# The last stretch of a fused attention and soft-MoE kernel, with its value products, transposes and one polynomial chain in another order

## The chip, the core and the metric

The kernel runs on one core of one Trainium2 chip. A core has five engines that work side by side, each through its own queue in program order: TensorE (PE in the profile; its weight loads, PEld, overlap its products), VectorE (DVE), ScalarE (ACT), GpSimd (POOL) and SyncE (SP), which only issues transfers. They wait for each other by semaphores. Data lies in SBUF (128 partitions) and matrix products land in PSUM, 8 banks of 2 KB a partition. The metric is the device time of one execution in microseconds (us); the kernel before takes 281.48, the median of 3 runs (281.21 to 282.12).

## What is computed

```
scores = q @ k.T / sqrt(64)                 # 8 batches x 12 heads, 448 x 448
scores = cap * tanh(scores / cap)           # cap = 30
attn   = softmax(scores) @ v
x      = attn, heads side by side           # 3584 rows x 768
logits = x @ phi                            # 3584 x 32 slots (8 experts x 4)
slot_input = softmax(logits, over rows).T @ x
slot_out   = relu(slot_input @ w1[e]) @ w2[e]     # per expert, 768 -> 1024 -> 768
out    = softmax(logits, over slots) @ slot_out
```

The slot sums go over all rows, so no expert product can start before the last head's attention is done; and all 11 MB of the output follow the experts.

## The kernel before, in words

**Attention.** Heads go in pairs, 0 to 47, and two pairs make a quad. Scores are kept transposed: a tile is 64 keys of both heads of a pair (128 partitions) by 448 queries, and a pair has 7 tiles. All 336 tiles stand in one list and are worked off in 56 chunks of 6. For a chunk j the PE makes scores (`qk_chunk`, in two halves of 3 tiles), ScalarE makes tanh of each half (`tanh_chunk`) and one exp over the chunk (`exp_chunk`). For many chunks the first tiles' exp is done on VectorE instead, by a polynomial of seven steps (`poly_exp`, L602 to L609); the table `SHARED` says how many tiles (one for chunk 54), the table `POLY` at which slot each step is issued. The steps of a chunk depend on each other in order.

Value products (`pv_mms`, L613 to L629) take exp tiles as stationary operand and the values, with a column of ones, as moving one. The 448 queries are 3 groups of 128 and a rest of 64. The groups are products of form 128\*128; the rest goes as two products of form 64\*64, one per head ("tail products"). `norm` (L631) divides by the sums (a reciprocal, then a multiply, both VectorE) into `xq`. `x_transp` (L682) transposes a pair's `xq` on PE into a PSUM tile `xps` (3 transposes of form 128\*128, 2 of form 64\*64; there is one buffer for all users of `psT`) and copies it to `xT`. `phi_last` (L960) multiplies `xT` with phi into the logits `lpl` (again 3 of full form, and for the rest two of form 128\*64).

**Order.** The order on every engine is written out by hand. Each chunk j of the main loop (L893 on) has named slots ("0", "m", "e", "a", "b", "r", "c", "d"), each with a "<" part before and a ">" part after; `at(j, slot, f, ...)` puts a piece of work in one. `spare` and `busy` are PE products of ones without use for the result. The last chunk, 55, takes exp in three pieces, of 3, 2 and 1 tiles (L930 to L932).

**The end.** `TAILSEQ` (L991) is the order of what follows the main loop: "m" and "mt" are pair 46's group and tail products (into `pvm`), "nm" its normalization, "l" and "lt" pair 47's group and tail products (into `pvl`, two halves: groups 0 and 1, and group 2 with the rest), "n" the normalization of such a half, "x45" and "x46" those pairs' transposes (x46 with its copy on ScalarE), "p" phi products of a range of pairs. With CM = 2, tile CM of pair 46 is the one whose exp is the polynomial of chunk 54. C1, C2, C3 = 1, 4, 6: pair 47's tile 0 is in chunk 54, tiles 1 to 3, 4 to 5 and 6 belong to the three exp pieces. `turns` (L941) gives the PSUM banks in order of use. Then `x_last` transposes pair 47's two halves into `xpl`, `phi_last` adds the last phi products, `e_last` takes exp of the logits in two halves, `slot_mms` makes the slot sums, and `layer1` (L1064) begins the experts.

**Transfers.** SyncE's queue first loads values, then 21 parts of w2 (`w2t`, L1049) into memory that attention has given up, then stores the output (L1126).

Of the kernel before, what the change touches and what calls it, by code (L numbers as in the profile page):

```python
# [10 lines left out]
BF16 = mybir.dt.bfloat16  # L11
# [7 lines left out]
P = 128  # L19
HP = 64  # L20
NT = 7
# [16 lines left out]
def kernel(  # L38
# [12 lines left out]
    B, H, _, _ = q.shape  # L51
# [11 lines left out]
    NQ = B * NQB  # L63
# [6 lines left out]
    pe, dve, act, pool, sp = nc.tensor, nc.vector, nc.scalar, nc.gpsimd, nc.sync  # L70
# [3 lines left out]
    psT = ctx.enter_context(tc.tile_pool(name="psT", bufs=1, space=PSUM))  # L74
# [301 lines left out]
    def exp_chunk(j):  # L376
# [199 lines left out]
            (54, '<a'): ((53, 4),),  # L576
            (54, '<b'): ((54, 0), (53, 5)),
            (54, '>b'): ((54, 1),),
            (54, '>c'): ((53, 6),),
            (55, '0'): ((54, 2),),  # L580
            (55, 'e'): ((54, 3),),
            (55, '<a'): ((54, 4),),
            (55, '>a'): ((54, 5), (54, 6))}
    shared = dict(SHARED)

    octaves = cap * math.log2(math.e)
# [73 lines left out]
    def pv_tail(pr, c0, c1):  # L660

        pv_mms(pr, c0, c1, (NF,), pvs[pr][:, 2 * NF:NT, :])
# [125 lines left out]
    def at(j, slot, f, *a):  # L788
        if j < 0:
            j, slot = 0, "b"  # L790
        aux.setdefault((j, slot), []).append((f, a))
# [9 lines left out]
    def quad_in(Q, cast_k, cast_q, k_in, q_in, v_in):  # L801
        if 0 < Q < NQ:
            for nm, when in (("k", cast_k), ("q", cast_q)):
                at(*when, *((cast, nm) if Q == 1 else (load, nm, Q + 1)))
            at(*k_in, transp, "k", Q)
            at(*q_in, transp, "q", Q)
            if Q == 1:
                for n in range(2):
                    at(*v_in, vcast, Q, n)
# [6 lines left out]
    for b in range(B):  # L816
        j, p = b * PER, 6 * b

        def when(nm):
            return j + WHEN[nm][0], WHEN[nm][1]  # L820

        if b == 0:
            quad_in(1, (0, "c"), (0, "c"), (0, "d"), (0, "d"), (2, "d"))
        else:
            quad_in(3 * b + 1, *(when(x + "1") for x in ("lk", "lq", "k", "q", "v")))
        for n in (2, 3):
            quad_in(3 * b + n, *(when(f"{x}{n}") for x in ("lk", "lq", "k", "q", "v")))
        if b == 0:
            at(j + 1, "d", spare, 14)
            at(j + 2, "d", spare, 5)  # L830
        for k, slot, f, n in FILL:
            if (b or k > 2) and j + k < NCH - 1:
                at(j + k, slot, f, n)
        for hq in range(NQB if b < B - 1 else 1):
            at(*when(f"x{hq}"), x_transp, NQB * b + hq)
        if b == B - 1:
            at(j + 6, "a", x_transp, NQ - 2, (0,))
        if b < B - 1:
            at(*when("lg"), logits, b)
            at(*when("ee"), e_exp, b)  # L840
            at(*when("ss"), slot_sums, b)
            if b < B - 2:
                at(*when("et"), e_transp, b)
            if b % 2:
                at(*when("es"), e_sums, b // 2)
# [4 lines left out]
        at(1 + n * (NCH - 5) // len(wjobs), "b", *job)  # L850
    for j, slot, n, parts in ((0, "a", 5, 1), (0, "c", 16, 3), (1, "b", 12, 3), (1, "c", 3, 1)):
        at(j, slot, spare, n, parts)
    LATE = ((52, 'd', 3, 1), (54, 'd', 3, 3),)
    for j, slot, n, parts in LATE:
        at(j, slot, spare, n, parts)
    at(34, "<b", fill, 7)
# [15 lines left out]
    def busy(n, home=None, by=None):  # L872
        home, by = junk if home is None else home, ones if by is None else by
        if home.shape[-1] > P:
            for _ in range(n // 3):
                pe.matmul(home, ones, wide, start=True, stop=True)
            n, home = n % 3, home[:, 0:P]
        for _ in range(n):
            pe.matmul(home, by, by, start=True, stop=True)
# [47 lines left out]
    last = NPAIR - 1  # L927
# [10 lines left out]
    attp.close()  # L938
    mid = ExitStack()
    big = mid.enter_context(tc.tile_pool(name="big", bufs=1, space=PSUM, reuse_waits="tile"))  # L940
    turns = [0, 1, 2, 6, 3, 4, 5, 0, 6, 0, 1, 2, 3, 6, 5, 4, 0, 1, 2, 6, 3, 0, 1, 2, 6, 5]  # L941

    def bank(shape, dt=F32, name="bank"):
        n = turns.pop(0)
        return big.tile(shape, dt, name=name, tag=f"b{n}")
# [9 lines left out]
    CM = sum(place[last - 1, c] < NTILE - 2 * CH for c in range(NT))  # L955

    def pv_last(c0, c1, half, tails=(False, True)):
        pv_mms(last, c0, c1, halves[half], pv2[half], tails)

    def phi_last(pr, gs, done=False):  # L960
        Q, h = divmod(pr, 2)
        for g in gs:
            phi_mms(lps[g // 2][:, g % 2, :], xTs[Q][:, h, :], g, pr % NJ,
                    pr == last - 5 and g % 2 == 0, done)

    def tail_step(what, *a):
        if what == "m":
            pv_mms(last - 1, *a, (0, 1, 2), pvs[last - 1])
        elif what == "mt":
            pv_tail(last - 1, *a)  # L970
        elif what == "nm":
            norm(last - 1, 0, NT, pvs.pop(last - 1))
        elif what == "x45":
            x_transp(NQ - 2, (1,))
        elif what == "x46":
            x_transp(NQ - 1, (0,), act.copy)
        elif what == "l":
            pv_last(*a, (False,))
        elif what == "lt":
            pv_last(*a, 1, (True,))  # L980
        elif what == "p":
            for gs in ((0, 1, 2), (NF,)):
                for pr in range(*a):
                    phi_last(pr, gs)
        elif what == "n":
            norm(last, cuts[a[0]], cuts[a[0] + 1], pv2[a[0]])
        else:
            run(NCH - 1, what)

    C1, C2, C3 = NT - CH, NT - CH + CL, NT - 1  # L990
    TAILSEQ = (("m", 0, CM), ("m", CM, NT), ("l", 0, C1, 0), ("x45",), ("mt", CM, NT),  # L991
               ("mt", 0, CM), ("l", 0, C1, 1), ("l", C1, C2, 0), ("p", last - 5, last - 1), ("l", C2, C3, 0),
               ("nm",), ("l", C3, NT, 0), ("l", C2, C3, 1), ("l", C3, NT, 1), ("l", C1, C2, 1),
               ("x46",), ("lt", C3, NT), ("n", 0), ("lt", C2, C3), ("lt", C1, C2),
               ("lt", 0, C1), ("n", 1))
    for step in TAILSEQ:
        tail_step(*step)
    assert not aux, aux.keys()

    el = consts.tile([P, NG, NS], BF16, name="E", tag="E", bufs=2)  # L1000
    es[bl] = el
    xpl = [bank([P, 2 * P], BF16, name="xpl"),
           psT.tile([P, 2 * P], BF16, name="xpl", tag="T")]
    zl = bank([P, NS], name="zps")

    def x_last(s, copy):
        q0, q1 = 2 * s * P, min(2 * s * P + 2 * P, S)
        turn_x(xpl[s], q0, last, halves[s])
        copy(xTs[NQ - 1][:, 1, q0:q1], xpl[s][:, 0:q1 - q0])

    def e_last(s):
        act.activation(el[:, 2 * s:2 * s + 2, :], lps[s], ACT.Exp)

    busy(1)
    x_last(0, act.copy)
    busy(3)
    phi_last(last - 1, (0, 1, 2))
    x_last(1, dve.tensor_copy)
    phi_last(last, (0, 1), True)
    busy(6)  # L1020
    e_last(0)
    phi_last(last, (2,))
    phi_last(last - 1, (NF,))
# [150 lines left out]
    for n in range(B // 2 * NT):  # L1174
        bb, c = divmod(n, NT)
# [59 lines left out]
```

## Time and profile before

| | |
|---|---|
| median of 3 runs | 281.48 us (281.21 to 282.12) |
| span of the profiled execution | 279.2 us (the page does not give its whole time) |
| busy: PE, DVE, ACT, POOL | 247.0, 239.1, 248.6, 142.0 us |
| last exp piece of attention ends | 235.40 us |
| first expert product | 239.63 us |
| first store issued | 249.98 us |
| granted clock, 228 to 270 us | 1.00 |

One execution is profiled; times are counted from its first instruction. In rows in order of time the columns are start, time from the first start to the last end, engine, line, operation, tiles written and read, form and shape, count, and in brackets the idle time before it and what ended it. Rows of the same kind that follow each other are merged. A matmul's row ends when its result is there; the next one may issue long before.

### The profile page before, as it was taken

The page shows a single profiled execution, that of the slowest core. Times are in us where ns is not written, and L with a number is a line of the kernel's source. Part 1 is how long each engine was busy: PE and PEld are TensorE (multiplying, and loading weights), DVE is VectorE, ACT ScalarE, POOL GpSimd, SP SyncE. Part 2 cuts the span into 40 slices and gives each one's busy share as a digit, 9 for nine tenths or more (in the row PEclk, how much of TensorE's full clock was granted, in tenths as well). Part 3 has the DMA queues.
Part 4 walks back from the last instruction along what each step waited for, and adds up shares of the span by engine and source line. Part 5 has one row for each costly group of instructions (what it writes and reads, how often), then busy time and mean ns, then how long its engine had stood idle before and what let it go on. Part 6 is the DMA issues. An engine that isn't in the chain of part 4 may idle for free.

```text
span 279.2 us, 10421 instructions
## 1 busy us (share of the span) xinstructions
PE 247.0 (88%) x4560; PEld 166.6 (60%) x4560; DVE 239.1 (86%) x473; ACT 248.6 (89%) x195; POOL 142.0 (51%) x198
## 2 busy tenths in 40 slices
PE   8898989998999999989999999899999999998720
PEld 7555556756675766566756675657566678553300
DVE  3479999999999999999999999999999997347940
ACT  4999999999999999999999999999999998237720
POOL 8796548662957296728673758375743230200000
PEclk9999999999999999999999999999999999999995
DMA  6999999999999999999999999999999588979997
GB/s 197 277 193 202 219 219 234 229 221 219 224 225 220 219 229 226 225 217 229 223 226 212 213 219 231 218 210 215 231 217 215 117 279 293 367 290 383 434 424 312
DMA packets 57340, 68.08 MB, mean 244 GB/s; under 512 B 4048, under 2 KB 53840, under 8 KB 56784
## 3 DMA queue, kind: packets, MB, share of 16 engines
q0 software_dynamic: 42448, 35.31, 80.0%
q1 hardware_dynamic: 14704, 32.02, 32.6%
q8 instruction: 35, 0.57, 0.7%
q10 hardware_dynamic: 144, 0.10, 0.1%
q14 instruction: 9, 0.07, 0.1%
HBM read 91.72 MB, written 19.27 MB: 398 GB/s over the span
## 4 chain that ended last, share of the span: by engine, by line
ACT 38%; DVE 27%; PE 27%; issue 3%; POOL 1%; ACTq 0%; DVEq 0%
ACT ex L366 15%; ACT ex L374 15%; PE pv L627 8%; ACT ex L362 6%; DVE xq L637 4%; PE sc L349 3%; DVE xp L605 3%; DVE xp L607 3%; DVE ex L608 2%; DVE ex L602 2%; PE so_ps L1098 2%; PE hp L1070 2%; DVE xf L604 2%; DVE ex L609 2%; DVE xp L606 2%
## 5 line engine op out<-in xcount | busy, mean ns | idle before, releaser
L366 ACT ACTIVATE ex<-sc 128x1344 f16<-128x1344 f32 (+1 forms) x87 | 112.9, 1402 | 0.9 <-PE sc L349 0.9
L374 ACT ACTIVATE ex<-ex 128x1344 bf16<-128x1344 f16 (+5 forms) x58 | 110.7, 1916 | 0.1
L627 PE MATMUL pv<-vbd,ex 128*128 128x130 bf16 (+1 forms) x1610 | 94.0, 212 | 7.6 <-POOL vbd L289 3.4
L627 PEld LDWEIGHTS <-ex 128*128 128x128 bf16 (+1 forms) x1680 | 75.6, 101 | 34.9 <-issue 6.2
L289 POOL CAST vbd<-vraw 64x896 bf16<-64x896 f32 x46 | 47.3, 1028 | 57.3 <-PE pv L627 35.7
L349 PE MATMUL sc<-qT,kT 64*64 64x448 bf16 x672 | 66.0, 359 | 6.7 <-ACT ex L366 4.8
L362 ACT ACTIVATE ex<-sc 128x2688 f16<-128x2688 f32 x13 | 33.6, 2586 | 0.0
L349 PEld LDWEIGHTS <-kT 64*64 64x64 bf16 x672 | 22.1, 105 | 16.3 <-ACT ex L366 6.9
L637 DVE TENSOR_TENSOR xq<-pv,rec 128x448 bf16<-128x448 f32 x46 | 28.7, 625 | 1.6
L607 DVE TENSOR_TENSOR xp<-xp,xf 128x1344 f16<-128x1344 f16 (+2 forms) x34 | 27.1, 798 | 0.6
L608 DVE TENSOR_TENSOR ex<-ex,xp 128x1344 uint16<-128x1344 uint16 (+2 forms) x34 | 26.9, 791 | 0.2
L605 DVE TENSOR_TENSOR xp<-xf 128x1344 f16<-128x1344 uint16 (+2 forms) x34 | 26.8, 789 | 0.2
L116 POOL DMA_DIRECT2D w1b<-in_moe_w_dram x32 | 26.3, 825 | 0.0
L602 DVE TENSOR_SCALAR ex<-ex 128x1344 uint16<-128x1344 f16 (+2 forms) x34 | 17.0, 500 | 1.4 <-ACT ex L366 0.8
L606 DVE TENSOR_SCALAR xp<-xp 128x1344 f16<-128x1344 f16 (+2 forms) x34 | 17.2, 505 | 0.6
L281 DVE COPY kT<-kps 128x896 bf16<-128x896 bf16 x23 | 14.2, 617 | 4.0 <-PE kps L276 2.8
L297 POOL MEMSET vbd<- 64x1 bf16 x22 | 2.8, 129 | 28.6 <-PE pv L627 28.3
L604 DVE TENSOR_SCALAR xf<-ex 128x1344 uint16<-128x1344 uint16 (+2 forms) x34 | 16.7, 491 | 0.4
L185 POOL DMA_DIRECT2D qb<-in_q_dram x22 | 16.3, 740 | 1.2 <-PE qps L279 0.5
L609 DVE TENSOR_SCALAR ex<-ex 128x1344 uint16<-128x1344 uint16 (+2 forms) x34 | 16.4, 483 | 0.4
L120 POOL DMA_DIRECT2D w2d<-in_moe_w_dram x21 | 16.4, 816 | 0.0
L185 POOL DMA_DIRECT2D kb<-in_k_dram x22 | 16.3, 739 | 0.0
(124 smaller groups left out, 320.2 us busy)
## 6 DMA issues: line engine op xcount, KB each, us to landing
w1b<-in_moe_w_dram POOLq DMA_DIRECT2D x32, 384.0 KB, 10.2
vraw<-in_v_dram SPq DMA_DIRECT2D x44, 224.0 KB, 6.2
w2d<-in_moe_w_dram POOLq DMA_DIRECT2D x21, 384.0 KB, 9.9
w2t<-w2d SPq DMA_DIRECT2D x21, 384.0 KB, 6.2
qb<-in_q_dram POOLq DMA_DIRECT2D x22, 224.0 KB, 8.2
kb<-in_k_dram POOLq DMA_DIRECT2D x22, 224.0 KB, 8.1
w2b<-in_moe_w_dram POOLq DMA_DIRECT2D x11, 384.0 KB, 9.5
out_dram<-ob SPq DMA_DIRECT2D x2, 1536.0 KB, 7.7
```

The costliest lines, as they stand in the source:

```text
L116: pool.dma_start(out=w1b[e][:, js, fs], in_=w1r[:, e, js, fs])
L185: pool.dma_start(out=t, in_=quad_ap(nm, Q))
L289: pool.tensor_copy(vbds[Q % 2][r, :, :, c0:c0 + DH], raw[r])
L349: ins = pe.matmul(sc[cs, u, 0:S], qkT["k", Q][r, c, cs], qkT["q", Q][r, :, cs], start=True, stop=True).ins
L362: apart["t", i - 1] = apart["t", i] = act.activation(exs[j].bitcast(F16), own["board"][:, :, 0:S], ACT.Tanh, scale=qk_scale / cap).ins
L366: ins = act.activation(exs[j][:, half * CS + u0:half * CS + u1, :].bitcast(F16), (own[0] if i == u0 == 0 else sc)[:, u0:u1, 0:S], ACT.Tanh ...
L374: act.activation(exs[j][:, u0:u1, :], exs[j][:, u0:u1, :].bitcast(F16), ACT.Exp, scale=cap)
L605: lambda: dve.tensor_tensor(p, s, s.bitcast(F16), op=ALU.mult),
L607: lambda: dve.tensor_tensor(p, p, s, op=ALU.mult),
L608: lambda: dve.tensor_tensor(y, y, p, op=ALU.add),
L627: pe.matmul(out_, exs[j][r, u, q0:q0 + (HP if tail else P)], v_, start=(c == 0 and g == gs[0] < NF), stop=(c == NT - 1), skip_group_check= ...
L637: dve.tensor_tensor(xq[Q][:, h, s0:s1, :], pv[:, 0:s1 - s0, 0:DH], rec.to_broadcast([P, s1 - s0, DH]), op=ALU.mult)
```

## The change

- The last polynomial step of chunk 53 and those of chunk 54 are issued one or two slots sooner; pair 44's transposes come after pair 45 instead of between its products.
- The spare product at (54, 'd') is left out, and of `busy(1)`, `busy(3)`, `busy(6)` at the end only one `busy(1)` stays, at another place.
- `TAILSEQ` is new: pair 46's polynomial tile is last of its group products; pair 46's normalization comes before pair 47's later products; pair 47's tail products go in two groups (tiles 0 to 3, then 4 to 6); x46 and the phi products come at the end. The phi products of pairs 44 and 45 are issued between the two `x_last`.
- `x_last(0)` copies on VectorE and `x_last(1)` on ScalarE instead of the reverse; the second `xpl` is in bank 3 instead of the `psT` buffer.

```
-            (54, '>c'): ((53, 6),),
-            (55, '0'): ((54, 2),),
-            (55, 'e'): ((54, 3),),
-            (55, '<a'): ((54, 4),),
-            (55, '>a'): ((54, 5), (54, 6))}
+            (54, '<c'): ((53, 6), (54, 2)),
+            (54, '>c'): ((54, 3),),
+            (55, '0'): ((54, 4),),
+            (55, 'e'): ((54, 5),),
+            (55, '<a'): ((54, 6),)}
...
-            at(j + 6, "a", x_transp, NQ - 2, (0,))
+            at(j + 6, "t0", x_transp, NQ - 2, (0,))
...
-    LATE = ((52, 'd', 3, 1), (54, 'd', 3, 3),)
+    LATE = ((52, 'd', 3, 1),)
...
-    turns = [0, 1, 2, 6, 3, 4, 5, 0, 6, 0, 1, 2, 3, 6, 5, 4, 0, 1, 2, 6, 3, 0, 1, 2, 6, 5]
+    turns = [0, 1, 2, 6, 3, 4, 5, 0, 3, 6, 0, 1, 2, 3, 6, 5, 4, 0, 1, 2, 6, 3, 0, 1, 2, 6, 5]
...
-    TAILSEQ = (("m", 0, CM), ("m", CM, NT), ("l", 0, C1, 0), ("x45",), ("mt", CM, NT),
-               ("mt", 0, CM), ("l", 0, C1, 1), ("l", C1, C2, 0), ("p", last - 5, last - 1), ("l", C2, C3, 0),
-               ("nm",), ("l", C3, NT, 0), ("l", C2, C3, 1), ("l", C3, NT, 1), ("l", C1, C2, 1),
-               ("x46",), ("lt", C3, NT), ("n", 0), ("lt", C2, C3), ("lt", C1, C2),
-               ("lt", 0, C1), ("n", 1))
+    TAILSEQ = (("m", 0, CM), ("m", CM + 1, NT), ("m", CM, CM + 1), ("l", 0, C1, 0), ("x45",),
+               ("mt", 0, NT), ("nm",), ("l", 0, C1, 1), ("l", C1, C2, 0), ("l", C1, C2, 1),
+               ("lt", 0, C2), ("l", C2, C3, 0), ("l", C2, C3, 1), ("l", C3, NT, 0), ("n", 0),
+               ("l", C3, NT, 1), ("lt", C2, NT), ("n", 1), ("x46",), ("p", last - 5, last - 3))
...
-    xpl = [bank([P, 2 * P], BF16, name="xpl"),
-           psT.tile([P, 2 * P], BF16, name="xpl", tag="T")]
+    xpl = [bank([P, 2 * P], BF16, name="xpl") for _ in range(2)]
...
+    x_last(0, dve.tensor_copy)
+    tail_step("p", last - 3, last - 1)
+    x_last(1, act.copy)
+    phi_last(last - 1, (0, 1, 2))
+    phi_last(last, (0, 1), True)
     busy(1)
-    x_last(0, act.copy)
-    busy(3)
-    phi_last(last - 1, (0, 1, 2))
-    x_last(1, dve.tensor_copy)
-    phi_last(last, (0, 1), True)
-    busy(6)
     e_last(0)
     phi_last(last, (2,))
```

## The prediction

> **What bounds the kernel now.** I read the head of the page, then the engines' busy time stage by stage, then each engine's rows in order of time from the last stretch of attention to the first expert product, and last the store queue. Times are microseconds from the span's start; the columns of the stages are the stretch, its length, busy time (instructions) of PE, weight loads, VectorE, ScalarE, GpSimd, then granted clock, DMA share, GB/s.
>
> ```profile
> span 279.2 us, 10421 instructions
> 229.70:232.25 2.55, 2.49 (x43) 1.87 (x42) 2.48 (x7) 2.55 (x3) 0.03 (x1) 1.00 0.91 309
> 232.25:235.40 3.15, 3.15 (x75) 2.89 (x72) 2.17 (x7) 3.15 (x4) 0.00 (x0) 1.00 0.85 280
> 235.40:239.63 4.23, 4.21 (x84) 3.12 (x82) 1.72 (x7) 1.32 (x5) 0.18 (x1) 1.00 0.89 309
> 239.63:250.00 10.37, 10.37 (x228) 5.95 (x228) 4.77 (x18) 2.91 (x5) 1.63 (x1) 1.00 0.91 359
> 260.00:270.00 10.00, 5.29 (x26) 2.26 (x24) 7.45 (x9) 5.84 (x7) 0.00 (x0) 1.00 1.02 426
> ```
>
> ScalarE is busy 2.55 of 2.55 and 3.15 of 3.15 until 235.40: it sets the pace of attention's last stretch. From 235.40 it is idle two thirds of the time and a chain through PE, VectorE and ScalarE sets the pace, with PE issuing nearly throughout (4.21 of 4.23). From 239.63 PE alone does (10.37 of 10.37), until stores begin; then the DMA engines are full (1.02). The pieces that the change touches lie between these rows:
>
> ```profile
> 234.72 0.68 ACT L374 ACTIVATE ex<-ex 128x448 bf16<-128x448 f16 x1
> 234.67 0.46 PE L694 MATMUL lpl<-phib,xT 128*128 128x32 bf16 x12
> 235.06 0.30 PE L698 MATMUL lpl<-phib,xT 128*64 128x32 bf16 x8
> 235.29 0.86 PE L627 MATMUL pvl<-vbd,ex 128*128 128x130 bf16 x12
> 235.99 0.33 PE L675 MATMUL xps<-ident,xq 128*128 128x128 bf16 x3
> 236.25 0.22 PE L680 MATMUL xps<-ident,xq 64*64 64x64 bf16 x2
> 236.30 0.39 PE L627 MATMUL pvl<-vbd,ex 64*64 64x65 bf16 x14
> 235.84 0.18 DVE L634 RECIPROCAL rec<-pvl 128x4 f32<-128x4 f32 x1 [0.53 <-PE pvl L627]
> 236.06 0.42 DVE L637 TENSOR_TENSOR xq<-pvl,rec 128x256 bf16<-128x256 f32 x1
> 236.73 0.18 DVE L634 RECIPROCAL rec<-pvl 128x3 f32<-128x3 f32 x1 [0.24 <-PE pvl L627]
> 236.94 0.36 DVE L637 TENSOR_TENSOR xq<-pvl,rec 128x192 bf16<-128x192 f32 x1
> 237.36 0.23 PE L675 MATMUL xpl<-ident,xq 128*128 128x128 bf16 x1
> 237.52 0.22 PE L680 MATMUL xpl<-ident,xq 64*64 64x64 bf16 x2
> 237.78 0.26 DVE L1009 COPY xT<-xpl 128x192 bf16<-128x192 bf16 x1 [0.48 <-PE xpl L680]
> 238.09 0.19 PE L694 MATMUL lpl<-phib,xT 128*128 128x32 bf16 x1
> 238.49 0.22 ACT L1012 ACTIVATE E<-lpl 128x64 bf16<-128x64 f32 x1 [0.35 <-PE lpl L698]
> 239.63 4.07 PE L1070 MATMUL hp<-w1b,slT 128*32 128x512 bf16 x72
> ```
>
> So the last exp piece ends at 234.72 + 0.68 = 235.40. The path from it: last value products, the tail products (236.30 to 236.69), normalization of the last half (236.73 to 237.30), its transposes (237.36 to 237.74), VectorE's copy (to 238.04), the last phi products (238.09), exp of the logits (to 238.71), slot sums, and the first expert product at 239.63, which is 4.23 after the exp. Everything before 235.40 counts only if it delays PE beyond that moment.
>
> ```profile
> L1098 PE MATMUL so_ps<-w2t,hpad x84: 326/326/336, 247.4 to 252.9; 128*32 128x384 bf16 x84
> L1049 SPq DMA_DIRECT2D w2t<-w2d x21: 319/371/1539, 222.2 to 242.5; - x21
> DMA to landing us min/median/max: 3.0/6.2/8.5
> 249.98 8.86 SPq L1126 DMA_DIRECT2D out_dram<-obh  x16
> ```
>
> Does a shift at 239.63 reach the end? The last w2t load is issued at 242.5 and lands by 242.5 + 8.5 = 251.0 at the latest; its products are the last of the 84, near 252.9, so PE does not wait for it. The first store, at 249.98, follows PE's work; from then on the stores run at full DMA share. A shift under about 1 us is thus passed on one for one, sooner or later.
>
> **The change part by part.** First the two prices. A 130-column value product issues every (0.86 - 0.23) / 11 = 0.058, taking one matmul's 0.23 off its row of 12; a phi product every (0.46 - 0.19) / 11 = 0.025; a pair of tail products about (0.39 - 0.22) / 6 = 0.03. A change of form (full rows to 64 rows or columns, or back): the 3 transposes at 235.99 should issue in 0.17, and the next form begins after 0.26, so 0.09; the 12 phi products 0.30, after 0.39, again 0.09; the 8 narrow ones, in pairs 0.035 apart, 0.14, after 0.23, again 0.09.
>
> The Trainium skill, "TensorEngine Tiling (Array Packing)", section "Tiling Modes", says that a change of tiling mode drains the TensorE. The rows agree that a change costs, 0.09 each; by a full drain, taken as one matmul's 0.22, it would be more than twice that, which is the second rival below.
>
> *Product left out, spare at (54, 'd').*
>
> ```profile
> 229.75 0.34 PE L876 MATMUL junk<-ones 128*128 128x384 bf16 x1
> 230.14 0.90 PE L627 MATMUL pv<-vbd,ex 128*128 128x130 bf16 x12
> 229.07 0.62 DVE L637 TENSOR_TENSOR xq<-pv,rec 128x448 bf16<-128x448 f32 x1
> ```
>
> Pair 45's products can start at 229.69 + 0.06 = 229.75 instead of 230.14: 0.39 sooner on PE. ScalarE is the bound there, so this is worth 0 by itself.
>
> *Polynomial steps one place sooner, pair 44's transposes after pair 45.*
>
> ```profile
> 231.29 0.39 DVE L607 TENSOR_TENSOR xp<-xp,xf 128x448 f16<-128x448 f16 x1
> 231.59 0.38 DVE L689 COPY xT<-xps 128x448 bf16<-128x448 bf16 x1
> 231.90 0.38 DVE L608 TENSOR_TENSOR ex<-ex,xp 128x448 uint16<-128x448 uint16 x1
> 232.50 0.20 DVE L634 RECIPROCAL rec<-pv 128x7 f32<-128x7 f32 x1
> 232.74 0.62 DVE L637 TENSOR_TENSOR xq<-pv,rec 128x448 bf16<-128x448 f32 x1
> ```
>
> VectorE runs the same operations; the copy of pair 44 (0.31 of the queue) goes behind pair 45's normalization, and L608 then follows L607 directly, which I price at +0.12 (L608 to its dependent successor L609 is 0.41 against the 0.30 from L607 to the copy). So the reciprocal is at 232.50 - 0.31 + 0.12 = 232.31, xq ends near 233.17 and the copy near 233.47. Pair 45's transposes use the same PSUM tile, so PE is held there until 233.47 + 0.06 = 233.53 (now they run near 233.6). From there to the last piece PE has: transposes 0.22, 14 tail products 0.21, 10 value products 0.58, 8 tail products 0.12, 6 value products 0.35, and 5 changes 0.45, sum 1.93, ready at 235.46. The exp piece releases PE at about 235.45. So this part costs 0, with no reserve: every 0.1 that VectorE is later there is 0.1 later at the end. I bound it by 0 and +0.2 (half of that 0.41).
>
> *Order behind the last exp.* From 235.45 on PE issues: 3 value products 0.17, 6 tail products 0.10, pair 46's transposes 0.22, phi of pairs 42 and 43 0.22, first transposes of pair 47 0.12, phi of 44 and 45 0.22, one transpose 0.06: 1.11 of work, and 9 changes of form, 0.81. The last pair of transposes then issues at 235.45 + 1.92 = 237.37 (now 237.52). VectorE is no longer what is late: the last half's tail products issue by 235.80 and end by 236.0, the first half's normalization (0.18, 0.42) occupies VectorE from 235.76 (its last product, issued at 235.51, ends by 235.73) to about 236.35, so the second ends near 236.90 instead of 237.30 and waits 0.3 for PE. The phi products, 0.44 plus four changes 0.36, were under ScalarE's exp before; now they stand on PE's path and eat most of the 0.40 won. The junk between (L876, L879) goes and had filled waits; it is worth 0.
>
> *Copies exchanged.*
>
> ```profile
> 236.51 0.53 ACT L689 COPY xT<-xps 128x448 bf16<-128x448 bf16 x1 [1.10 <-PE xps L680]
> 237.00 0.37 ACT L1009 COPY xT<-xpl 128x256 bf16<-128x256 bf16 x1
> ```
>
> The last copy, 192 columns, moves from VectorE (0.26) to ScalarE: between 0.37 at 256 columns and 0.53 at 448 the slope gives 0.32; bounds 0.26 and 0.37. So: last transposes end 237.37 + 0.22 = 237.59, copy 237.63 to 237.95, phi at 238.00 instead of 238.09. The second xpl in a bank of its own frees it from pair 46's copy; both bank owners (pvm, pvl) have been read by then, so 0. Behind 238.00 nothing changes.
>
> Sum: 0 + 0 - 0.09 = -0.09 at the first expert product, hence at the end. The profiled execution's whole time is not on the page; the median stands 281.48 - 279.2 = 2.3 above the span, which I take as what lies around it. Forecast 281.48 - 0.09 = 281.39, so 281.4.
>
> **The rivals.**
> *PE is lighter than I sum* (form changes partly hidden behind weight loads): then VectorE's result decides, the single transpose issues at 236.96 instead of 237.36, and with 0.06 given back by the slower copy the gain is 0.34: 281.1. For it: weight loads are busy only 3.12 of 4.23; against it: the three rows all showed 0.09. It also bounds the gain of this order: the rest of the path is unchanged.
>
> *PE's queue behind the last exp becomes the bound* (slower). Twelve changes of form stand from the exp to the slot sums instead of six, nine of them ahead of the last transposes. If a change where the next operand also comes fresh costs a whole result time, 0.22, then 9 x 0.13 = 1.17 is added, less 0.09: +1.08, 282.6. It decides from 0.10 a change upward, and passes +0.84 from 0.19. For it: the new changes sit between very short groups (2 to 6 products), which no row shows in such density. Against it: 0.09 thrice.
>
> *The clock falls without the junk* (slower): the 4.07 of L1070 would at worst double, 285.5. Against it: between 260 and 270 PE is busy only 5.29 of 10 and the clock is 1.00. By the Trainium skill, "TensorE: Matmul & The Clock Gate", section "Part 1: The HAM clock gate", an idle window of about 3.4 us halves the clock; no gap of that length arises here.
>
> *It doesn't reach the end.* If the w2t stream, landing up to 251.0, rather than the store at 249.98 sets the start of the stores, any gain is lost: 281.5.
>
> **How the numbers follow.** My forecast has 0.50 (its own range 281.1 to 281.7), lighter PE 0.13, lost gain 0.13, PE's queue 0.11, the clock 0.03. The other 0.10 is for a gain outside this path, which I can't name: this order yields 0.34 at most. A difference of 0.3%, 0.84, is about what a measurement of this kernel can tell from none. Same: 0.50 + 0.13 + 0.13 = 0.76; slower 0.11 + 0.03 = 0.14; faster 0.10. The range, with the runs' own 281.21 to 282.12 and half of the queue's case, is 280.8 to 282.3; it leaves out the unnamed gain, the clock and the worse half of the queue's case, some 0.19.
>
> **What would show it.** Right: L374's last piece still ends near 235.4; VectorE's last xq ends near 236.9; the last L680 pair issues near 237.4, with PE and not VectorE as what it followed; the last copy is on ScalarE with 0.32; L1070 begins near 239.5 and the first store near 249.9. Wrong: L374's last piece ends elsewhere (then something reaches ScalarE that I did not see); gaps over 0.15 at changes of form (second rival); pair 45's L675 later than 233.7 (the shared PSUM tile); a clock below 1.00 before 270; or the first store's shift not found again in the span.

## The result, and the profile after

The changed kernel takes 282.45 us, the median of 22 runs (281.87 to 285.57); the kernel before, run beside it, 281.7 (22 runs, 280.76 to 282.56). The ratio is 1.0037, 95% interval 1.0022 to 1.0052. The change makes the kernel slower by a third of a per cent, about 1 us, where 281.4 and no measurable difference had been forecast.

The rows of the changed kernel's trace that answer to those of before, each engine's in order of time (its line numbers are smaller by 3 from `layer1` on: L1067 was L1070, L1095 was L1098, L1123 was L1126):

```profile
232.93 2.73 ACT L374 ACTIVATE ex<-ex 128x1344 bf16<-128x1344 f16 x3
236.81 0.36 DVE L637 TENSOR_TENSOR xq<-pvl,rec 128x192 bf16<-128x192 f32 x1
237.73 0.22 PE L680 MATMUL xpl<-ident,xq 64*64 64x64 bf16 x2
237.99 0.32 ACT L1007 COPY xT<-xpl 128x192 bf16<-128x192 bf16 x1 [0.72 <-PE xpl L680]
239.90 5.59 PE L1067 MATMUL hp<-w1b,slT 128*32 128x512 bf16 x72
251.78 8.85 SPq L1123 DMA_DIRECT2D out_dram<-obh  x16
```

The last exp piece ends at 232.93 + 2.73 = 235.66, 0.26 later than before. Executions of one kernel differ by that much: four traces of the changed kernel end it between 235.61 and 235.95, and take 229.62 to 230.20 from the first score product to it (two of before: 229.68 and 229.81). From there to the first expert product it is 4.24, against 4.23. So the new order neither won nor lost. The first 72 expert products then take 5.59 instead of 4.07, and the first store comes 251.78 - 239.90 = 11.88 behind the first expert product instead of 10.35. From the store to the end it is 29.2 in both. The stages show what the 1.5 us are (stretch, its length, PE, weight loads, VectorE, ScalarE, GpSimd, granted clock, DMA share, GB/s):

```profile
235.40:239.63 4.23, 4.10 (x89) 3.24 (x87) 1.38 (x6) 1.47 (x5) 0.00 (x0) 1.00 1.01 392
239.63:250.00 10.37, 10.37 (x205) 5.78 (x208) 4.68 (x18) 1.86 (x3) 1.81 (x1) 0.84 0.84 335
260.00:270.00 10.00, 7.08 (x40) 3.31 (x37) 9.19 (x11) 7.41 (x9) 0.00 (x0) 1.00 1.04 425
```

The clock is 0.84 on average in the second stretch, where it was 1.00. The same view in stretches of 3.41, which is the step at which the trace's clock record changes:

```profile
236.21:239.62 3.41, 3.28 (x77) 2.66 (x74) 1.21 (x6) 1.21 (x4) 0.00 (x0) 1.00 1.02 406
239.62:243.03 3.41, 3.41 (x38) 1.43 (x40) 1.31 (x6) 0.00 (x0) 1.81 (x1) 0.50 1.03 408
243.03:246.44 3.41, 3.41 (x84) 1.89 (x76) 1.24 (x3) 1.38 (x2) 0.00 (x0) 1.00 1.03 412
```

One whole step, 239.62 to 243.03, ran at half clock, over the first expert products. Such a step at 0.50 is called a half-clock step in what follows. The step ahead of it counts as 3.28 busy of 3.41: PE was issuing, but products of 32 to 128 columns.

That is one execution. The same kernel, traced a second time, kept the full clock and was still longer than before, by another loss. The two losses have to be told apart: the clock, which fits the first profile, is not the whole story.

### The profile page after: what moved, and what is told of

Same layout as the page of the kernel before. It is cut to its first block, busy times and chain, and to the rows that moved or that the text cites. A ratio compares the mean times of both kernels' runs of the same rounds, so it can differ in the third digit from the quotient of the medians.

```text
span 281.0 us, 10414 instructions
## 1 busy us (share of the span) xinstructions
PE 248.3 (88%) x4556; PEld 166.8 (59%) x4556; DVE 240.3 (86%) x473; ACT 248.6 (88%) x195; POOL 142.0 (51%) x198
## 4 chain that ended last, share of the span: by engine, by line
ACT 32%; PE 28%; DVE 28%; issue 4%; DMA 2%; POOL 1%; SPq 0%; ACTq 0%; DVEq 0%
ACT ex L374 13%; ACT ex L366 12%; PE pv L627 8%; ACT ex L362 6%; PE sc L349 4%; DVE xq L637 4%; DVE xp L605 3%; DVE xp L607 3%; PE hp L1067 2%; DVE ex L608 2%; DVE ex L602 2%; PE so_ps L1095 2%; DVE qT L281 2%; DVE xf L604 2%; DMA qraw<-in_q_dram 2%
## 5 line engine op out<-in xcount | busy, mean ns | idle before, releaser
L602 DVE TENSOR_SCALAR ex<-ex 128x1344 uint16<-128x1344 f16 (+2 forms) x34 | 18.2, 535 | 1.4 <-ACT ex L366 0.8
```

## The experiments

In what follows a trace is broken down at the end of the last exp piece, at the first expert product and at the first store. "Fill" is the products of ones between the last pieces (`busy`), which nobody reads. The changed kernel keeps one of 128 columns there; the kernel before has one of 128, then one of 384, then two of 384.

### Which part of the change

Front alone, twice: the kernel before with the earlier polynomial steps, pair 44's transposes later and the spare product left out; its end and fill are those of before.

```
-            at(j + 6, "a", x_transp, NQ - 2, (0,))
+            at(j + 6, "t0", x_transp, NQ - 2, (0,))
...
-    LATE = ((52, 'd', 3, 1), (54, 'd', 3, 3),)
+    LATE = ((52, 'd', 3, 1),)
```

> The kernel before with only the front part of the change: polynomial steps sooner, pair 44's transposes behind pair 45, the spare at (54, 'd') left out. TAILSEQ and all after it are old. Theory W: pair 45's products end sooner and release the eighth load sooner, so 44.2 to 45.0 us from the last exp's end, ratio 1.001 to 1.004. Rival (the new order of the end costs): 43.7 to 43.9 us, ratio 0.999 to 1.001.

> e6 once more, for its ratio and a second trace. Both theories: 0.997 to 1.000, 43.7 to 44.1 us from the last exp's end, the clock at full until 268 us; if it is 1.000 or more, the gain seen in e6 was a draw of its runs.

Ratios 0.9984 (0.9968 to 1.0001) and 0.9998 (0.9981 to 1.0014). From the exp to the first expert product it is 4.17 and 4.18, then 10.35 to the first store and 29.2 to the end: the front part costs nothing, and wins 0.05 at most. The loss that the first expectation gave it (1.001 to 1.004) did not come.

End alone: the changed kernel with that part undone (old `POLY`, transposes at "a", spare kept). Spare back: the changed kernel with the spare product at (54, 'd') kept.

> The changed kernel with the front part undone: the new TAILSEQ, copies, banks and the one busy(1) at the end, but the old polynomial places, pair 44's transposes in slot a and the spare product at (54, 'd'). Theory W: the eighth load is released as before, 43.7 to 44.0 us from the last exp's end unless the clock falls (then 1.5 more), ratio 0.999 to 1.002. Rival (the new order of the end costs): 44.3 to 45.4 us, ratio 1.002 to 1.005.

> The changed kernel with only the spare product at (54, 'd') put back (one 384-column product near 229.7). Theory (the clock at the end): this product lies over 6 us ahead of the weak stretch and changes nothing: ratio 1.002 to 1.006 like the changed kernel. Rival (this left-out product is what held the clock or the pace): ratio 0.999 to 1.001.

End alone 1.0014 (0.9994 to 1.0033), spare back 1.0016 (1.0000 to 1.0033). Both ratios lie below the 1.002 that a costly end was expected to show, and their intervals reach 1, so these runs alone don't settle it. The traces do: both have the full clock, and both are longer from the exp to the end than before (43.79, and 44.07 in its second trace): 44.35 and 44.47. The loss lies in the end, not in the front, and not all of it is clock. (Of the 0.68 in spare back 0.19 comes ahead of the first expert product; why stays open.)

### The same kernels again

> The kernel before once more, for a second trace in its own order. Both theories: ratio 0.999 to 1.001; from the last exp's end to the end of the span 43.8 us within 0.1, no idle time of PE marked issue inside L1098's products and no half-clock interval before 268 us. If it shows either, the stalls are not the change's own but come in some executions of both kernels, and only their share of the runs differs.

> The changed kernel once more, for a second trace. Theory (the clock): ratio 1.002 to 1.006; the trace shows either a half-clock interval of 3.41 us that begins between 236 and 241 us, or none, and then L1067's 72 products take 4.1 us and the span is 1.3 to 1.8 us shorter than 281.0. Rival (the order costs): span near 281 without any such interval.

> The changed kernel, one more look for another phase of the clock window. Clock theory: the first 72 expert products take about 5.6 us if the window begins 0 to 1.4 us after the last exp, and about 4.1 us otherwise. Rival (contention for the w2 transfers slows these products): no relation to the phase.

> The changed kernel, a further look for another phase: as for the third, 5.6 us for the first 72 expert products if the clock window begins 0 to 1.4 us after the last exp, 4.1 us otherwise.

Before again: 0.9994 (0.9977 to 1.0011); its trace takes 44.07 from the exp to the end, where 43.8 within 0.1 was expected, the 0.27 more in the stores. Changed again: 1.0027 (1.0010 to 1.0043); the third and the fourth are single executions of 282.07 and 283.96. Two of the four traces of the changed kernel have the half-clock step (the first and the last), two have not; the span of the second is 280.2, 0.8 shorter than the first one's, where the clock alone was to make it 1.3 to 1.8 shorter. The row of the last, and its step:

```profile
240.19 5.75 PE L1067 MATMUL hp<-w1b,slT 128*32 128x512 bf16 x72
236.97:240.38 3.41, 3.28 (x76) 2.62 (x78) 1.24 (x7) 1.20 (x4) 0.37 (x1) 1.00 1.02 377
240.38:243.79 3.41, 3.41 (x36) 1.36 (x32) 0.80 (x4) 0.00 (x0) 1.44 (x1) 0.50 1.03 406
```

The second trace of the changed kernel, with the full clock (start, time, engine, line, in brackets the idle time ahead):

```profile
239.85 4.07 PE L1067 MATMUL hp<-w1b,slT 128*32 128x512 bf16 x72
247.65 1.31 PE L1095 MATMUL so_ps<-w2t,hpad 128*32 128x384 bf16 x28
249.31 0.51 PE L1095 MATMUL so_ps<-w2t,hpad 128*32 128x384 bf16 x8 [0.35 <-issue]
```

and the same place before:

```profile
247.43 1.64 PE L1098 MATMUL so_ps<-w2t,hpad 128*32 128x384 bf16 x36
249.00 0.50 PE L1138 MATMUL op<-so,ET 128*128 128x384 bf16 x2
```

The 4.07 is back, but where the kernel before runs 36 products on end, PE stops behind the 28th for 0.35 and what follows starts 0.53 late (9.47 behind the first expert product, against 8.94). "Issue" says that it waited for nothing that the profile shows: no semaphore, no transfer of data. So there are two losses, in different executions: 1.5 by the clock, and some 0.5 here and a bit later.

### Fill and clock

Fill back in the changed kernel, as two products of 384 columns in the wait ahead of the logits' exp:

```
-    busy(1)
+    busy(6)
```

> The changed kernel with busy(6) instead of busy(1) at its one place: two 384-column products of ones in the wait before the last phi product (238.05 to 238.36 in the changed kernel's trace). Theory (the clock): in a stretch of 3.41 us before the first expert product the products stream too few columns, the clock is halved for the next 3.41 us; the columns streamed in the weakest such stretch rise from 0.34 of what a full clock can stream to 0.42, and the fill costs no time because PE waits there. The clock falls in fewer runs or none: ratio to the kernel before 0.999 to 1.002. Rival (the order of the end itself costs, by its changes of form on PE's queue): the fill changes nothing or costs 0.1 us: ratio 1.003 to 1.006.

The kernel before without its fill but for one product of 128 columns, twice:

```
-    busy(1)
     x_last(0, act.copy)
-    busy(3)
...
-    busy(6)
+    busy(1)
```

> The kernel before, in its own order, with busy(1) and busy(3) left out and busy(6) cut to busy(1). Theory (the clock): the weakest 3.41 us stretch falls from 0.52 to about 0.37, the clock is halved in a part of the runs and L1070's 72 products then take 5 to 6 us instead of 4.07: ratio 1.002 to 1.006. Rival (the order costs): the order is the old one and the junk stood in waits, so ratio 0.999 to 1.001.

> The kernel before without the filled waits, once more. Clock theory: with the old order the streamed share of a 3.41 us stretch falls below 0.40 for about four tenths of all phases, so about four executions in ten lose 1.5 us: median 0.3 to 0.7 us above before, ratio 1.001 to 1.0025, and in the profiled execution 5.6 us for the first 72 expert products if its clock window begins between 0 and 1.4 us after the last exp, 4.1 us otherwise. Rival (the fill is worth nothing, the new order alone is slow): ratio 1.0000 within 0.001, and 4.1 us whatever the phase.

Fill back: 1.0014 (0.9997 to 1.0031), clock full; its trace is nevertheless as long from the exp to the end (45.29) as the changed kernel's first (45.33), by the other loss (last table). Before without fill: 1.0005 (0.9989 to 1.0022), then 1.0027 (1.0005 to 1.0048). The first of these is a miss for the theory, which had 1.002 or more; the second lies above 1. Neither trace has a half-clock step at the end, but neither tests the place where the changed kernel loses its clock: a step begins 2.71 behind the exp in the first and 1.83 behind it in the second.

The traces side by side. Column 2: where the 3.41 us step that decides begins, behind the last exp. Column 3: the share of that step in which the array had columns to stream, at 0.16 us for 384 columns. The 0.16 is from five fill products in a row near the start of the changed kernel, (0.99 - 0.34) / 4, taking a single one's 0.34 off:

```profile
9.89 0.99 PE L876 MATMUL junk<-ones 128*128 128x384 bf16 x5
```

| trace | step begins | streamed share | next step |
|---|---|---|---|
| changed | 0.54 | 0.33 | half clock |
| changed, fourth | 1.02 | 0.34 | half clock |
| changed, fifteenth transfer held | 1.05 | 0.34 | half clock |
| changed, pages moved | 1.06 | 0.34 | half clock |
| changed, eighth transfer held | 1.32 | 0.40 | half clock |
| fill back; hold and fill | 0.70, 0.70 | 0.37, 0.37 | full |
| end alone; spare back | 1.54, 1.68 | 0.42, 0.42 | full |
| front alone; before | 0.85, 1.46 | 0.44, 0.48 | full |
| changed again; changed third | 2.04, 2.03 | 0.53, 0.53 | full |

Products that stream side by side count once here; the expectations counted each in full, so their shares are higher. The traces that the table leaves out have 0.47 or more and the full clock.

In nine traces, the new end without fill loses its clock whenever a step begins 0.5 to 1.4 behind the exp, and not otherwise; with fill it kept it at 0.70, and at 1.36 in the kernel with pages moved and fill (below). The share doesn't order the table strictly (0.40 lost, 0.37 didn't), so it is near what the clock goes by, not the thing itself.

Over all runs: each lists its mean clock; one half step lowers it by 1.7 / 281 = 0.006, and traces without one show 0.981 to 0.987. A count at 0.980 is rough, since the first trace of the changed kernel has a half step and 0.981, and since a half step elsewhere counts too. At 0.980 or below were 5 of 82 runs of kernels with fill (old end 2 of 47, new end 3 of 35), 2 of 139 of the kernel before that ran beside them, and 25 of 102 without fill (old end 6 of 24, new end 19 of 78). Where steps begin 0.5 to 1.4 behind the exp in 0.9 of 3.41 us, an estimated 0.26 of the executions should lose the clock, and 19 of 78 is 0.24. The two kernels with pages moved are not in these counts: their ends run 1.7 longer at half clock, which lowers the mean by itself (0.980 or below in 3 of 6 runs and, with fill, in 4 of 12).

For the new end, traces and counts agree that leaving the fill out is what costs the clock. For the old end the counts alone say so, and the one low run of it that was traced had lost its clock in the middle of attention instead.

### Are the w2 transfers late or early?

The new end frees memory in another order, so w2 parts are issued at other times. Two kernels hold one part back (the eighth, until pair 45's last value product; the fifteenth, until a phi product of pair 43), one adds the fill to the latter, and one lets the fifteenth go early in the front-alone kernel, by moving one group of tail products ahead of the last exp pieces.

```
+        if (n0, half) == (36, 1):
+            tc.add_manual_dep(ins, held.name, ...)
```
```
-               ("mt", 0, CM), ("l", 0, C1, 1), ("l", C1, C2, 0), ("p", last - 5, last - 1), ("l", C2, C3, 0),
+               ("mt", 0, CM), ("l", 0, C1, 1), ("lt", 0, C1), ("l", C1, C2, 0), ("p", last - 5, last - 1), ("l", C2, C3, 0),
...
-               ("lt", 0, C1), ("n", 1))
+               ("n", 1))
```

> The changed kernel; the eighth load of w2t (SyncE's queue waits there, so all that follow too) is held until pair 45's last value product, which puts it 3.9 us ahead of the last exp's end as in the kernel before instead of 4.5. Theory W (w2 loads that start sooner fill the transfer queues when PE's code and the first stores need them): code loads come as early as before, no idle time of PE marked issue inside L1095, the time from the last exp's end to the end of the span is 43.7 to 44.0 us instead of 44.5 to 45.4, ratio 0.999 to 1.001. Rival (the order of the end itself, or the clock): unchanged, 44.5 to 45.4 us and ratio 1.002 to 1.005.

> The changed kernel; the fifteenth load of w2t, which takes the place of chunk 54's exp tiles, is held until pair 43's full phi products have ended, 1.3 us after the last exp's end, where the old order released it (the new one reads chunk 54 for the last time before the last exp, and issues this load at +0.5 to +1.1). Theory V (the earlier release fills the transfer queue in front of PE's code loads): code loads begin 4.2 to 4.6 and 10.2 to 10.6 us after the exp's end as in the old order, no idle time marked issue inside L1095, 43.7 to 44.1 us from the exp's end to the end of the span unless the clock falls (+1.5), ratio 0.999 to 1.002. Rival (this load does not matter): code loads at 4.7 to 5.9 and 10.9 to 12.6, 44.4 us or more, ratio 1.001 to 1.005.

> The kernel of e6 (old order of the end, which took 43.7 us from the last exp's end) with one move: the tail products of pair 47's tile 0, the last readers of chunk 54, go from the end to before the last exp. Theory V: the fifteenth load starts at +0.4 to +1.1 instead of +1.31, code loads come later (4.7 or more, 10.9 or more), 44.2 to 45.0 us, ratio 0.2 to 0.4% above that of e6. Rival (this load does not matter): 43.7 to 43.9 us, ratio as e6.

> e9 with busy(6) instead of busy(1) as in e1: both suspected losses taken away, the new order of the end kept. Theory V with the clock: 43.7 to 44.1 us from the exp's end, no half-clock interval before 268 us, ratio 0.998 to 1.001. Rival (the new order costs in another way): ratio 1.001 to 1.004.

> The changed kernel with the fill back in its wait and the fifteenth w2 transfer held. Clock theory: granted clock 1.00 throughout whatever the phase, first 72 expert products 4.1 us, ratio 1.000 to 1.001. Rival (the earlier 1.0002 was chance): ratio 1.002 or more, as of the kernel that only holds the transfer.

The edits moved the parts: the eighth is issued 3.64 ahead of the exp's end instead of 4.5, the fifteenth 1.35 behind it instead of 0.27 to 1.05 (three traces of the changed kernel), and with early release at 0.03 instead of 1.31. Eighth held 1.0057 (1.0030 to 1.0084), fifteenth held 1.0037 (1.0022 to 1.0051): no better than the change. Early release 1.0005 (0.9984 to 1.0026), 43.84 from the exp to the end against 43.73 and 43.72 of front alone. When these transfers start is not the cause. Fifteenth held and fill back: 1.0002 (0.9984 to 1.0020), and again 1.0010 (0.9990 to 1.0031). The two kernels with the fifteenth held ran on the same chip in one go and differ in `busy(6)` alone, with intervals that don't meet; the interval of the second measurement alone would not exclude 1.002. With the fill and the fifteenth held the trace still takes 44.38 from the exp to the end, where 43.7 to 44.1 was expected, and the stop near the 28th product stays:

```profile
239.09:242.50 3.41, 3.41 (x64) 1.71 (x65) 1.55 (x7) 0.41 (x1) 1.81 (x1) 1.00 1.03 408
248.63 0.66 PE L1101 MATMUL so_ps<-w2t,hpad 128*32 128x384 bf16 x9 [0.23 <-issue]
```

(fifteenth held and fill, first run: the step that runs at half clock in the changed kernel, at 1.00, and the stop).

### The stop: PE waits for its own code

With the fifteenth held and the fill, the stop stands behind 27 products of the 36, one sooner than in the changed kernel. PE has one product more ahead of that place there. So the stop stays at one place of the instruction stream, not of the work. The page has a queue that fits, first of the changed kernel:

```profile
PE 248.3 (88%) x4556; PEld 166.8 (59%) x4556; DVE 240.3 (86%) x473; ACT 248.6 (88%) x195; POOL 142.0 (51%) x198
...
q8 instruction: 35, 0.57, 0.7%
```

35 packets, 0.57 MB: 16 KB each, for 2 x 4556 instructions; PE starts 4326 products between the first packet and the last, 127 to a packet, so a packet holds some 128 products with their weight loads, or 256 instructions: a page of code. (The two kernels below with 87 products more have 36 packets.) At the stop and the two places 128 and 256 products ahead of it a packet begins 0.4 to 4 us behind the place, as if PE, on entering a page, had the next one fetched. (Only the last packet of those two kernels begins 0.3 and 0.9 ahead of its place.) Before has 4560 products: four more, so its page ended four products sooner, behind the 204th expert product instead of the 208th.

To test it, all fill products of 384 columns well ahead of the change were split in three or four with the same columns in sum. That adds 87 products and puts the page ends elsewhere; one kernel without, one with the fill at the end.

```
             for _ in range(n // 3):
-                pe.matmul(home, ones, wide, start=True, stop=True)
+                for c in range(0, 3 * P, 96 if n > 10 else P):
+                    pe.matmul(home[:, c:c + (96 if n > 10 else P)], ones,
+                              wide[:, c:c + (96 if n > 10 else P)], start=True, stop=True)
```

> The changed kernel with its filler products of 384 columns, all of them well before the changed stretch, split into three or four with the same columns in sum: PE has 174 more instructions, so the boundaries of its 256-instruction code pages lie about 87 products earlier, at the 7th product before the first expert product and the 122nd behind it, instead of at the 209th. Code theory (PE waits for its next page of code at the 209th product): no idle time marked issue there, the first store 10.35 to 10.4 us behind the first expert product where the clock stays full, and a ratio of 1.001 to 1.002, what the clock still takes. Rival (the new order's w2 transfers hold that product): the idle time stays at the 209th product, first store 10.7 to 10.9 behind, ratio 1.0025 to 1.004.

> The same with the two 384-column filler products back in the wait ahead of the logits' exp (split in three each), page boundaries at the 12th product before the first expert product and the 117th behind it. Both theories together (clock and code page): full clock throughout, no idle time at the 208th product, first store 10.35 to 10.4 us behind the first expert product, ratio 0.998 to 1.0005, which is as fast as the kernel before or slightly faster. Rival as above: first store 10.7 to 11.3 behind, ratio 1.0005 to 1.002, as with the fill alone.

Pages moved: 1.0081 (1.0052 to 1.0111). Pages moved and fill: 1.0046 (1.0022 to 1.0070). Both ratios are misses. The stop is gone, as the code theory said (209th product at 8.94, first store 10.35 behind the first expert product with the full clock; in the other, at half clock, 12.04 with no idle time marked issue). But two other stretches are longer. Attention takes 230.5 and 230.6 from its first score product to the last exp, some 0.8 more than before; whether the added products or their pages cost that stays open. And from the first store to the end it is 30.9 in both, 1.7 more than before. There the moved pages had put a code packet into the stores. The DMA view, cut in 40 slices from just ahead of the stores (share in tenths, then GB/s), of before, 249 to 253:

```profile
DMA  9433000000000000005999999999999999999989
GB/s 348 184 154 123 31 0 31 31 31 31 0 0 0 0 0 0 0 0 230 353 445 384 384 400 353 445 399 384 369 369 445 369 399 354 384 445 353 415 323 415
q8 instruction: 1, 0.02, 1.5%
```

of the changed kernel's second trace, 249.76 to 253.76:

```profile
DMA  0000060000000000007999850269999999999989
GB/s 31 31 31 31 0 164 0 0 0 0 0 0 0 0 0 0 0 0 246 353 399 399 338 200 15 77 261 476 353 399 384 338 476 369 384 369 369 461 323 445
q8 instruction: 1, 0.02, 1.7%
```

and with pages moved and fill, 250.33 to 256.33:

```profile
DMA  0000000000006999999999200000000199999999
GB/s 0 0 0 0 0 0 0 0 0 0 0 0 256 509 358 389 338 410 338 348 399 358 93 0 0 0 10 10 10 10 20 51 348 399 420 328 451 369 379 420
q8 instruction: 1, 0.02, 1.9%
```

The view counts a packet at its start, so the lone 164 GB/s of the second fence is the code packet (16 KB in a slice of 0.1). Before, it runs from 249.02 to 250.00, on one engine, and is through when the stores' data begin to move at 250.8; they then run without a break. In the changed kernel it runs from 250.35 to 251.46; the stores begin at 251.56 and fall to 15 GB/s for a moment near 252.2. With pages moved it runs from 252.41 to 254.25, among the stores, and they stop from 253.8 on. From 254.24 to 255.05 the trace has store packets of 1.5 KB one at a time, 0.06 to 0.19 each: it looks as if one engine made up what the others had done, while these had nothing (the trace doesn't name the engine of a packet). The fourth store is issued at 252.72 and the fifth at 254.71, where else one goes every 0.5. PE is not what held them: its 275th, 278th and 281st products start 14.23, 15.24 and 16.27 behind the first expert product there, and 14.24, 15.24 and 16.27 before. The median time of a store to landing, in the same views, of before and of pages moved and fill:

```profile
out_dram<-obh SPq DMA_DIRECT2D x7, 192.0 KB, 2.0
```
```profile
out_dram<-obh SPq DMA_DIRECT2D x8, 192.0 KB, 3.5
```

So one packet of 16 KB, whose time counts for one engine, holds up a store stream that is spread over all 16. The traces in order of how long a PE code packet runs behind the first store's issue:

| trace | code packet ahead of the 209th product ends | 209th product | first store | code packet among the stores | store to end |
|---|---|---|---|---|---|
| before | 6.87 | 8.94 | 10.35 | 0.02 | 29.21 |
| front alone, and again | 7.07, 7.30 | 8.94 | 10.35 | 0.09, 0.36 | 29.20, 29.19 |
| before without fill, again | 7.50 | 9.04 | 10.61 | 0.41 | 29.20 |
| hold and fill | 7.79 | 9.35 | 10.92 | 0.48 | 29.23 |
| changed, third and second | 8.08, 8.00 | 9.47 | 10.89 | 0.69, 0.72 | 29.41, 29.44 |
| end alone | 7.90 | 9.13 | 10.70 | 0.70 | 29.40 |
| before, again | 7.18 | 8.94 | 10.35 | 0.79 | 29.48 |
| fill back | 8.42 | 9.75 | 11.32 | 0.92 | 29.73 |
| spare back | 7.35 | 8.94 | 10.37 | 0.93 | 29.68 |
| pages moved and fill | elsewhere | 8.94 | 10.35 | 1.84 | 30.96 |

Columns 2 to 4 count from the first expert product; all have the full clock. The three such traces that are not in the table have 0.01, 0.34 and 0.78 in column 5 and 29.20, 29.20 and 29.49 in column 6 (before without fill, early release, hold and fill again), and those that lost the clock fit too (0.25 and 29.20 for the fifteenth held, up to 1.71 and 30.86 for pages moved). Up to half a microsecond behind the first store's issue the packet costs nothing (the data begin to move 0.8 behind the issue), and beyond that the loss grows with it. Ahead of the stores, the 209th product follows 1.2 to 1.6 behind the end of its code packet as soon as that packet ends later than about 7.4. With it the second trace of the changed kernel is accounted for: attention 0.21 later, 0.01 to the first expert product, 0.54 at the page end, 0.23 in the stores, in sum 0.99; its span is 280.2 against 279.2. The whole runs say the same: those with a mean clock of 0.983 or more have a median of 282.29 for the changed kernel (23 of its runs), and 281.27 for the kernels with the old end and fill (44); 119 such runs of the kernel before beside them have 281.43.

Why the packet is late in the new end is shown in part. Two page ends ahead of the stop, PE of the changed kernel enters a page 2.33 ahead of the first expert product, and PE of the kernel before 2.94 ahead; in the new end the phi products are pressed together behind the transposes. The packet that PE then asks for begins 0.4 to 1.7 behind the first expert product, against 0.0 to 0.4 with the old end, and the one ahead of the 209th product follows some 6 later in either. The order does this, not the number of products: before without fill has three of the four products less, and enters at 2.94 too, with packets 0.07 and 0.08 behind the first expert product; fill back has three less than before as well, and enters at 2.33. Why a packet begins so long behind its page end, and not always equally, stays open. So does why the new end with fill (28 runs at full clock, median 281.75) is faster than without it (51 runs, 282.22) where the clock isn't lost. No kernel with the new end is free of both losses; the front part alone, 0.9984 and 0.9998, is the best of all, and not measurably faster than before.

## Why the prediction was wrong

**What bounds the kernel: right to the first expert product.** ScalarE's exp set the end of attention in both (235.40, 235.66), and the chain behind it is 4.24 against 4.23.

**Price of left-out spare, poly and pair 44: right.** Forecast 0 with a bound of 0.2; front alone measured 0.9984 and 0.9998, spare back no gain.

**Order and copies: right in kind, 0.10 off.** Forecast -0.09, measured +0.01. VectorE's last division ends at 237.17, 1.51 behind the exp (forecast 1.50), the last transposes issue at 2.07 behind it (forecast 1.97), ScalarE's copy takes the 0.32 that was interpolated. PE and not VectorE was what came last, as said. The change of form cost about what the three rows had shown: (237.73 - 235.66 - 0.05 - 1.11) / 9 = 0.10 each by the forecast's own sum. So neither the lighter PE nor the second rival's PE queue came true.

**The step that failed: "The junk between (L876, L879) goes and had filled waits; it is worth 0."** It looked at those products as work that hides in a wait, and asked only whether the wait got shorter. They did something else: they kept the array streaming in a stretch that is poor in columns. In the new end, without them, the clock is halved for one step wherever the step falls badly, and the first expert products take 1.5 to 1.7 more each time.

**"Behind 238.00 nothing changes" failed too, and not by the junk alone.** A shift at 239.63 would indeed have been passed on. What was missing is that the stretches behind it have lengths of their own, set by the clock and by the code's arrival, and neither stood in any row on which the sum rested. With the full clock the changed kernel is 0.54 longer to the first store, where PE waits for its next page of code, and 0.23 longer from there to the end. The fill doesn't give this back (fill back has 0.97 and 0.52), and the old end without fill loses at most 0.26 of it. So the wait for code comes with the new order; the loss among the stores can come with the old one too (0.27 in the second trace of before).

**The clock rival was named, and given 0.03.** Its kind was right, its size 1.5 to 1.7 and not 4.07. The argument against it, that PE is only 5.29 of 10 busy from 260 to 270 and keeps its clock, compared idle time. But those products stream 384 columns each (26 of them at 0.16, so 0.42 of the time), and here PE was 3.28 of 3.41 busy with products of 32 to 128 columns. Busy time doesn't see the difference; the columns do. By the Trainium skill, "TensorE: Matmul & The Clock Gate", section "Part 1: The HAM clock gate", the window is about 3.4 us long and free-running, and an idle one halves the clock. The trace agrees on the length (3.41) and on the free run (its place differs from execution to execution); what it adds is that a window need not be idle, since one that was issuing for 3.28 of 3.41 was enough.

**The code pages stood in no rival.** By the Trainium skill, "Runtime: NRT & Kernel Launch", section "Instruction fetch mechanics", code comes in blocks of 16 KiB, 256 instructions, and crossing a block is mostly hidden. The 16 KB agree with 0.57 MB in 35 packets; hidden it was before, and in the changed kernel it cost 0.5 at one block and 0.2 at the next.

## What to carry to other kernels

Before a filler product is left out of a tight kernel, count the columns that the array streams in each stretch of 3.41 us without it, at the worst phase, and not the busy time. Where the order changes, look in the trace also for where PE's code pages end, whether the packet for the next page is through by then, and which packet meets the stores. And take more than one profile of the changed kernel where the difference is under 1%: the first one here showed one loss of two.

## What the runs showed of the hardware

A single 16 KB packet of PE's code takes 0.95 us in the median (0.88 to 2.17 over the 702 packets of all traces). Behind the first store's issue it sets the whole store stream back: 0.9 of it cost 0.5 at the end, and 1.84 cost 30.96 - 29.21 = 1.75, with the stream down from about 400 GB/s to between 0 and 10 for over a microsecond behind the packet.

The clock can fall in the middle of attention as well. The second run of the kernel before without fill, which is the same program as before up to that place, has:

```profile
199.54:202.95 3.41, 2.17 (x35) 1.18 (x32) 3.38 (x8) 3.41 (x4) 2.88 (x5) 1.00 1.26 230
202.95:206.37 3.42, 3.42 (x39) 1.48 (x38) 3.35 (x8) 2.91 (x2) 1.17 (x2) 0.50 1.25 230
```

PE was 2.17 of 3.41 busy there, and in the same stretch of the profiled execution of before 2.74, with the clock kept. The last exp of this execution ended at 238.66, some 3 us late, so a part of that kernel's 1.0027 may not be the edit's.
